# Attention bias of a fused three-stage kernel: two small loads issued ahead of a table, two scalings moved into the first block, 44 instead of 26 warm-up transposes

## The chip, the cores and the metric

The kernel runs on one core of a Trainium2 chip. A core has a matrix engine (TensorE; PE in the profile, with its weight loads as PEld), three elementwise engines (VectorE or DVE, ScalarE or ACT, GpSimd or POOL) and SyncE (SP), which here issues every transfer of the 16 DMA engines. Each engine works through its own instructions in order and waits at semaphores for the others. Matmul operands come from the on-chip memory (SBUF), results go to eight PSUM banks. The metric is the device time of one execution in microseconds (us).

## The reference, cut to what matters

The change lies in the bias of the attention, the first of three stages. Two feed-forward networks follow and are not touched.

```python
B, H, S, D = 2, 8, 576, 64                       # batch, heads, positions, head size; hidden = 32
scores = scale * np.matmul(q, k.transpose(0, 1, 3, 2))
rel = (pos[:, None] - pos[None, :]).astype(np.float32)
psi_rel = np.log1p(np.abs(rel))
psi_i = np.log1p(np.maximum(pos[:, None].astype(np.float32), 1.0))
x = (psi_rel / psi_i)[..., None]
h = np.maximum(x @ w1 + b1, 0.0)
bias = h @ w2                                    # (S, S, H)
scores = scores + bias.transpose(2, 0, 1)[None]
attn = softmax(scores)                           # over the last axis
x = attn @ v, then _moe_ref(x), then _moe2_ref   # the two feed-forward stages
```

## The kernel before

**The bias.** A hidden unit of the bias network is on where `w1*psi_rel > -b1*psi_i`. The kernel therefore keeps a table `lw` with the logarithms of all 1151 distances, one copy per partition shifted for four groups of 32 partitions (4 row offsets times 32 hidden units), and multiplies it once by `w1` (`w1c`, one number per partition). The thresholds `thr` hold `psi_i`, multiplied once by `-b1` (`b1c`). For a group of rows, DVE compares a 576-wide window of `lw` with a column of `thr` and writes a 0/1 mask (L254); every fifth group instead has ACT write the sign (L264, four pieces issued during the four groups before it). PE multiplies the mask with a small matrix `wb` made from `w2`, `w1` and `b1` (eight 128x288 matmuls for a group of two masks, into a PSUM tile `bps` of which there are two), and ACT copies the result to the SBUF tile `ev` (L281, or L279 after a sign group).

**Blocks.** Five blocks of rows run one after another (`bias_rows(t)`, 16 groups each in the first four, 8 in the last). In block 0 the window never reaches below column 496 of `lw`, so only the part from `NEAR = 448` on is needed there. Blocks 1 to 3 need the part below `NEAR` as well, block 4 has a table of its own, `lw8`.

**After a block.** When its last `ev` is written, SP issues 16 transfers (L298) that rearrange `ev` into tiles `ba` and `bc`; DVE multiplies and adds these (L313, L317) between the masks of the next block, at fixed groups (the first one at group 5). The moves of a block wait for its last copy into `ev`.

**The start.** SP issues, in order, the loads of `w1c`, `w2c`, the upper part of `lw` (L119), `b1c`, `thr`, the lower part of `lw` (L122), `lw8` (L123), then the first row scales `xt`, q, k and v. ACT scales the upper part (L135), then the lower part (L141) and `lw8` (L142), before its first copy into `ev`. PE runs 26 transposes of the identity (L94) as soon as the identity exists; their result is not used. DVE and POOL make `wb` from `w1c`, `w2c` and `b1c` (L130 to L140), with DVE scaling `thr` (L136) in between.

**Order.** The schedule is written by hand: the instructions of an engine stand in the order of the code, and a wait of the first holds up all behind it.

Of the kernel before, what the change touches and what calls it, by code (L numbers as in the profile page):

```python
# [14 lines left out]
AF = mybir.ActivationFunctionType  # L15
# [42 lines left out]
def attention_then_two_ffn(ctx: ExitStack, tc: tile.TileContext, q, k, v, w1, b1, w2, w_in, w_out, ca, cb, probs, e_w1, e_w2, c_l, c_l8, c_p, c_x, out):  # L58
    nc = tc.nc
    act, dve, pool, pe, sp = nc.scalar, nc.vector, nc.gpsimd, nc.tensor, nc.sync  # L60

    def f32(ap):
        return ap.bitcast(F32)

    def mm(o, l, r, start, stop):
        pe.matmul(o, lhsT=l, rhs=r, start=start, stop=stop)  # L66
# [21 lines left out]

    ps = ctx.enter_context(tc.tile_pool(name="ps", bufs=2, space=PSUM))

    WARM = 26
    warm = ps.tile([P, 512], F32, tag="o", name="warm")
    for _ in range(WARM):
        pe.transpose(warm[:, :P], ident, ident)  # L94
# [11 lines left out]
    lw = bp.tile([P, LW_W], F32, name="lw")  # L106
    lw8 = bp.tile([P, LW8_W], F32, name="lw8")
# [3 lines left out]
    w1c = bp.tile([P, 1], F32, name="w1c")  # L111
# [3 lines left out]
    NEAR = S - P  # L115
    c_lb = c_l.unsqueeze(1).to_broadcast([4, 32, LW_W])
    sp.dma_start(w1c, w1.unsqueeze(2).to_broadcast([4, HID, 1]))
    sp.dma_start(w2c, w2.unsqueeze(0).to_broadcast([4, HID, H]))
    sp.dma_start(lw[:, NEAR:], c_lb[:, :, NEAR:])  # L119
    sp.dma_start(b1c, b1.unsqueeze(0).unsqueeze(2).to_broadcast([4, HID, 1]))  # L120
    sp.dma_start(thr, c_p.unsqueeze(1).to_broadcast([4, 32, NROWG]))
    sp.dma_start(lw[:, :NEAR], c_lb[:, :, :NEAR])  # L122
    sp.dma_start(lw8, c_l8.unsqueeze(1).to_broadcast([4, 32, LW8_W]))  # L123

# [12 lines left out]
    for par in range(2):  # L137
        for r in range(4):
            rows = slice(32 * r, 32 * r + 32)
            (dve if par == 0 else pool).tensor_copy(wb[rows, par, :, :, :, 4 * par + r], f32(wacr[rows]).rearrange("p a c (q h) -> p a c q h", q=2))  # L140
    act.activation(lw[:, :NEAR], lw[:, :NEAR], AF.Copy, scale=w1c)  # L141
    act.activation(lw8, lw8, AF.Copy, scale=w1c)  # L142

    half = bp.tile([P, 1], F32, name="half")
    ones = bp.tile([P, 1], F32, name="ones")
# [86 lines left out]
    def halves():  # L232
        pool.memset(ones, 1.0)
        for i in range(1, 4):
            pool.tensor_tensor(wsum, f32(wb[:, 0, 0]) if i == 1 else wsum, f32(wb[:, i // 2, i % 2]), ALU.add)
        hs = ps.tile([P, 512], F32, tag="t", name="hs")
        mm(hs[:, :1], wsum.rearrange("p a q r h -> p (a q r h)"), ones, True, True)
        act.activation(half, hs[:, :1], AF.Copy, scale=0.5)

    def bias_rows(t):  # L240

        ng = 16 if t < 4 else 8
        l = lw if t < 4 else lw8
        ev = (ev_odd if t % 2 else ev_even).tile([P, ng, S], F32, tag="ev", name="ev")
        sm = {}

        def window(g, par):
            i0, m = t * P + 4 * ng * par + g, 32 * t + ng * par + g
            return l[:, S - 1 - i0:2 * S - 1 - i0], thr[:, m:m + 1]

        def mask(g, par):
            mk = bp.tile([P, S], F32R, tag="mask", name="mask", bufs=4)
            win, at = window(g, par)
            dve.tensor_scalar(mk, win, at, None, ALU.is_gt)  # L254
            return mk

        def sign(g, i):

            par, hf = divmod(i, 2)
            if hf == 0:  # L260
                sm.setdefault(g, []).append(bp.tile([P, S], F32R, tag="sign", name="sign", bufs=2))
            win, at = window(g, par)
            j = slice(288 * hf, 288 * hf + 288)
            act.activation(sm[g][par][:, j], win[:, j], AF.Sign, scale=-1.0, bias=at)  # L264

        for g in range(ng):

            sc = ps.tile([P, 2, 512], F32, tag="s", name="bps")
            sgn = g in SGN[t]
            ms = sm.pop(g) if sgn else [mask(g, par) for par in range(2)]  # L270
            if t == 0 and g == 3:
                halves()
            for hf in range(2):
                for par in range(2):
                    for part in range(2):
                        mm(sc[:, hf, :288], wb[:, par, part].rearrange("p a q r h -> p (a q r h)"), ms[par][:, 288 * hf:288 * hf + 288], par + part == 0, par + part == 2)
            e_out = ev[:, g].rearrange("p (a j) -> p a j", a=2)
            if sgn:
                act.activation(e_out, sc[:, :, :288], AF.Identity, scale=-0.5, bias=half)  # L279
            else:  # L280
                act.activation(e_out, sc[:, :, :288], AF.Copy)  # L281
            for i in range(4):
                if g + 5 - i in SGN[t]:
                    sign(g + 5 - i, i)

            for f, rows, quad, h, n in WITH.get((t, g), ()):
                f(rows, quad, dve, slice(h, h + n))
        return ev
# [41 lines left out]
    for t in range(5):  # L330
        if t == 4:

            xts[4] = xp.tile([P, S], F32, tag="xt", name="xt")
            ev_ph.close()
            ev_even = ev_ph.enter_context(tc.tile_pool(name="ev_last", bufs=1))
        ev = bias_rows(t)
        if t == 0:
            for e in range(2):
                split_k(e, pool)
        if t < 4:  # L340
            for quad in range(2):
                for ac in range(2):
                    bias_move(t, ev, quad, ac)
        if 0 < t < 3:
            bias_x(t + 1)
# [668 lines left out]
```

## Time and profile before

| what | us |
|---|---|
| median of 3 timed runs (lowest, highest) | 966.3 (966.03, 969.66) |
| the profiled execution, its own time | 963.71 |
| its span, first to last instruction | 961.8 |
| block 0 of the bias: first mask to last copy into `ev` | 11.83 to 37.06 |
| PE busy | 878.7 (91% of the span) |
| DVE / ACT / POOL busy | 550.1 / 463.6 / 202.4 |

The bias takes about the first 145 us, the attention runs to about 345, the feed-forward stages fill the rest with PE nearly always busy. The page's share of busy time is a mean over these stages; the change lies in the first 40 us, where the engines wait for transfers and for each other.

### The profile page before, as it was taken

How to read it: one execution, taken by the hardware profiler on the slowest of the kernel's cores; microseconds unless marked ns; L12 is line 12 of the kernel's file. 1: busy time of each engine (PE TensorE's matmuls, PEld its weight loads, DVE VectorE, ACT ScalarE, POOL GpSimd, SP SyncE). 2: the span in 40 equal slices, each digit the busy share in tenths (PEclk: the TensorE clock that was granted, in tenths of full speed). 3: DMA queues.
4: the chain of work that ended last, by engine and by line, in shares of the span. 5: the costliest groups of instructions: out<-in, count | busy, mean ns of one | idle time of the engine just before them, and what ended most of it. 6: DMA issues, size and time to landing. Idle time of an engine off the chain costs nothing.

```text
span 961.8 us, 13043 instructions
## 1 busy us (share of the span) xinstructions
PE 878.7 (91%) x5012; PEld 821.6 (85%) x5012; DVE 550.1 (57%) x853; ACT 463.6 (48%) x772; POOL 202.4 (21%) x223
## 2 busy tenths in 40 slices
PE   6866876899999979998989989999999999999998
PEld 5865875799888979988989988998899899989987
DVE  3666776688989878888889971222223231331111
ACT  3735554589888767877867742232112111111100
POOL 3000003575554433454733200000000000000000
PEclk7978887799999989999999999999999999999999
DMA  4255556422241312222221122021101210110000
GB/s 103 68 141 145 174 199 195 118 64 65 58 97 29 111 44 88 88 88 88 89 88 44 48 62 68 1 70 62 44 1 64 68 44 1 45 44 12 22 33 33
DMA packets 72552, 69.90 MB, mean 73 GB/s; under 512 B 42412, under 2 KB 51116, under 8 KB 72492
## 3 DMA queue, kind: packets, MB, share of 16 engines
q1 hardware_dynamic: 72492, 69.09, 24.0%
q8 instruction: 39, 0.64, 0.3%
q14 instruction: 21, 0.17, 0.1%
HBM read 45.48 MB, written 2.36 MB: 50 GB/s over the span
## 4 chain that ended last, share of the span: by engine, by line
PE 53%; DVE 18%; DMA 11%; ACT 10%; issue 4%; SPq 3%; POOL 0%; DVEq 0%; ACTq 0%; POOLq 0%
PE hp L66 22%; PE op L66 20%; DMA ba<-ev 8%; PE bps L66 3%; DVE qd L903 2%; DVE narrow L426 2%; PE sc L66 2%; DVE u L904 2%; DVE narrow L424 2%; SPq L298 2%; DVE pq L521 2%; PE o L66 2%; ACT u L899 2%; DVE pt L562 2%; ACT narrow L420 2%
## 5 line engine op out<-in xcount | busy, mean ns | idle before, releaser
L66 PE MATMUL hp<-x,wi 128*128 128x384 f32 x1656 | 294.3, 335 | 13.8 <-DVE u L921 13.7
L66 PEld LDWEIGHTS hp<-x,wi 128*128 128x128 f32 x1656 | 287.3, 188 | 18.5 <-issue 16.7
L66 PE MATMUL op<-w,h_hi 128*128 128x512 f32 (+1 forms) x592 | 178.4, 384 | 0.0
L884 ACT ACTIVATE h_hi<-hp 128x768 fp32r<-128x768 f32 x48 | 39.1, 814 | 245.1 <-PE hp L66 245.1
L885 DVE SCALAR_TENSOR_TENSOR h_lo<-hp,h_hi 128x768 fp32r<-128x768 f32 x48 | 45.9, 957 | 154.9 <-ACT h_hi L884 154.9
L66 PEld LDWEIGHTS op<-w,h_hi 128*128 128x128 f32 x592 | 110.0, 188 | 21.4
L66 PE MATMUL bps<-mask,wb 128*128 128x288 f32 x472 | 84.1, 342 | 38.1 <-DVE mask L254 25.0
L66 PEld LDWEIGHTS bps<-mask,wb 128*128 128x128 f32 x472 | 78.2, 227 | 42.3 <-ACT ev L281 15.4
L66 PE MATMUL op<-w,h_lo 128*128 128x512 f32 (+1 forms) x296 | 113.7, 384 | 0.0
L66 PE MATMUL yp<-g_hi,w 128*128 128x384 f32 x384 | 101.7, 335 | 2.0 <-ACT y L868 1.6
L956 DVE SCALAR_TENSOR_TENSOR acc<-op,pr_sb,acc 128x512 f32<-128x512 f32 (+1 forms) x28 | 20.5, 732 | 112.8 <-PE op L66 112.8
L66 PEld LDWEIGHTS yp<-g_hi,w 128*128 128x128 f32 x384 | 69.7, 188 | 3.1 <-ACT y L868 2.2
L66 PE MATMUL sc<-ks,qs 128*128 128x288 f32 x320 | 64.8, 332 | 7.7 <-DVE nm L521 4.5
L66 PEld LDWEIGHTS op<-w,h_lo 128*128 128x128 f32 x296 | 55.6, 188 | 11.0
L66 PE MATMUL yp<-g_lo,w 128*128 128x384 f32 x192 | 64.2, 334 | 0.0
L254 DVE TENSOR_SCALAR mask<-lw,thr 128x576 fp32r<-128x576 f32 x118 | 56.7, 531 | 13.1 <-PE bps L66 12.3
L281 ACT ACTIVATE ev<-bps 128x576 f32<-128x576 f32 x59 | 38.3, 650 | 49.2 <-PE bps L66 36.4
L66 PEld LDWEIGHTS sc<-ks,qs 128*128 128x128 f32 x320 | 48.7, 203 | 14.2 <-DVE nm L521 8.0
L838 POOL TENSOR_TENSOR g_lo<-u,g_hi 128x768 fp32r<-128x768 f32 x24 | 45.4, 1890 | 70.3 <-ACT g_hi L837 59.3
L521 DVE CUSTOM_DVE_ANT_0 pq<-sc,ba 128x576 f32<-128x576 f32 x72 | 53.8, 749 | 8.2 <-PE sc L66 8.1
L531 ACT ACTIVATE pq<-pq,nm 128x576 f32<-128x576 f32 x72 | 55.4, 769 | 3.4 <-DVE nm L521 3.1
L562 DVE TENSOR_TENSOR pt<-tp,pt 128x512 fp32r<-128x512 f32 x72 | 49.3, 684 | 11.7 <-ACT pt L561 11.1
(130 smaller groups left out, 1276.6 us busy)
## 6 DMA issues: line engine op xcount, KB each, us to landing
stage<-in_moe_w_dram SPq DMA_DIRECT2D x32, 512.0 KB
ba<-ev SPq DMA_DIRECT2D x32, 288.0 KB
bc<-ev SPq DMA_DIRECT2D x32, 288.0 KB
words<-in_moe_w_in_dram SPq DMA_DIRECT2D x7, 1024.0 KB
words<-in_moe_w_out_dram SPq DMA_DIRECT2D x7, 1024.0 KB
raw_q<-in_q_dram SPq DMA_DIRECT2D x32, 128.0 KB
raw_k<-in_k_dram SPq DMA_DIRECT2D x16, 128.0 KB
raw_v<-in_v_dram SPq DMA_DIRECT2D x16, 128.0 KB
```

The costliest lines, as they stand in the source:

```text
L66: pe.matmul(o, lhsT=l, rhs=r, start=start, stop=stop)
L254: dve.tensor_scalar(mk, win, at, None, ALU.is_gt)
L281: act.activation(e_out, sc[:, :, :288], AF.Copy)
L298: sp.dma_start(dst[:, h], ev[r:r + 29:4])
L420: act.activation(st, hi.bitcast(F32), AF.Abs, scale=SHIFT)
L521: dve.tensor_tensor_reduce(out=self.row(u).rearrange("p (a j) -> p a j", a=2), in0=sc[:, :, :288], in1=bs.rearrange("p (a j) -> p a j", a= ...
L531: act.activation(self.row(u), self.row(u), AF.Exp, bias=least.pop((self.n, u)), scale=-1.0, accum_out=self.sm[b][:, u - 4 * b:u - 4 * b + 1])
L562: dve.tensor_tensor(lo, tp, f32(hi), ALU.subtract)
L838: pool.tensor_tensor(lo, u, f32(hi), ALU.subtract)
L884: act.activation(hi, h, AF.Relu)
L885: dve.scalar_tensor_tensor(out=lo, in0=h, scalar=0.0, in1=f32(hi), op0=ALU.max, op1=ALU.subtract)
L956: dve.scalar_tensor_tensor(out=acc[:, j, cols], in0=op, scalar=pr_sb[:, j, e:e + 1], in1=acc[:, j, cols], op0=ALU.mult, op1=ALU.add)
```

## The change

Three edits. The loads of `b1c` and `thr` are issued before the upper part of `lw` instead of after it. The scalings of the lower part of `lw` and of `lw8` leave the start and stand in block 0 behind the copies of groups 9 and 12. The number of warm-up transposes goes from 26 to 44.

```diff
-    WARM = 26
+    WARM = 44
...
     sp.dma_start(w2c, w2.unsqueeze(0).to_broadcast([4, HID, H]))
-    sp.dma_start(lw[:, NEAR:], c_lb[:, :, NEAR:])
     sp.dma_start(b1c, b1.unsqueeze(0).unsqueeze(2).to_broadcast([4, HID, 1]))
     sp.dma_start(thr, c_p.unsqueeze(1).to_broadcast([4, 32, NROWG]))
+    sp.dma_start(lw[:, NEAR:], c_lb[:, :, NEAR:])
     sp.dma_start(lw[:, :NEAR], c_lb[:, :, :NEAR])
...
-    act.activation(lw[:, :NEAR], lw[:, :NEAR], AF.Copy, scale=w1c)
-    act.activation(lw8, lw8, AF.Copy, scale=w1c)
...
                 act.activation(e_out, sc[:, :, :288], AF.Copy)
+            if t == 0 and g in (9, 12):
+                x = lw[:, :NEAR] if g == 9 else lw8
+                act.activation(x, x, AF.Copy, scale=w1c)
             for i in range(4):
                 if g + 5 - i in SGN[t]:
                     sign(g + 5 - i, i)
```

The lines of the code move by two, so L281 of before is L279 of after, and so on. SP's first transfers before (`lw_117` is `lw8`; the last number is the elements per partition):

```order
L117 DMA w1c<-in_w_dram 128x1x1
L118 DMA w2c<-in_w_dram 128x1x8
L119 DMA lw<-in_c_l_dram 128x1x703
L120 DMA b1c<-in_b_dram 128x1x1
L121 DMA thr<-in_c_p_dram 128x1x144
L122 DMA lw<-in_c_l_dram 128x1x448
```

And the same place after:

```order
L117 DMA w1c<-in_w_dram 128x1x1
L118 DMA w2c<-in_w_dram 128x1x8
L119 DMA b1c<-in_b_dram 128x1x1
L120 DMA thr<-in_c_p_dram 128x1x144
L121 DMA lw<-in_c_l_dram 128x1x703
L122 DMA lw<-in_c_l_dram 128x1x448
```

The upper part of `lw` has moved two places back; what follows it keeps its place. ScalarE's first instructions before, from the table load on:

```order
L71 ACT_TABLE_LOAD
L135 ACTIVATE lw<-lw,w1c 128x703
L141 ACTIVATE lw<-lw,w1c 128x448
L142 ACTIVATE lw_117<-lw_117,w1c 128x640
L281 ACTIVATE ev<-bps 128x576
L264 ACTIVATE sign<-lw,thr 128x288
```

In the changed kernel L279 follows L135 at once, and the two scalings stand here, in block 0 from the copy of group 9 on (`lw_135` is `lw8`, L277 the copy of a sign group):

```order
L279 ACTIVATE ev<-bps 128x576
L283 ACTIVATE lw<-lw,w1c 128x448
L277 ACTIVATE ev<-bps,half 128x576
L262 ACTIVATE sign<-lw,thr 128x288
L279 ACTIVATE ev<-bps 128x576
L262 ACTIVATE sign<-lw,thr 128x288
L279 ACTIVATE ev<-bps 128x576
L283 ACTIVATE lw_135<-lw_135,w1c 128x640
L262 ACTIVATE sign<-lw,thr 128x288
L279 ACTIVATE ev<-bps 128x576
L262 ACTIVATE sign<-lw,thr 128x288
```

Two pieces of the sign of group 15 and the copies of groups 13 to 15 now stand behind the scaling of `lw8`.

## Rows read from the trace of the kernel before

**Rows 1.** Chain of waits to 65 us: start us, length us, what.
```profile
18.61 0.64 ACT ev L281
19.30 1.38 PE bps L66 x8
...
37.08 0.71 SPq L298
```

**Rows 2.** Timeline after block 0: start us, us, engine line operation [idle before, releaser].
```profile
43.57 1.36 DVE L313 TENSOR_TENSOR ba<-ba,xt 128x1152 f32<-128x1152 f32 x1 [3.36 <-DMA ba<-ev]
...
129.57 3.50 SPq L298 DMA_DIRECT2D ba<-ev  x4
```

**Rows 3.** Windows: PE, PEld, DVE, ACT, POOL busy us, granted clock, DMA share, GB/s.
```profile
4.00:6.00 2.00, 2.00 (x11) 2.00 (x10) 0.23 (x1) 0.00 (x0) 0.00 (x0) 1.00 0.24 84
...
10.00:12.00 2.00, 0.00 (x0) 0.00 (x0) 1.64 (x9) 0.00 (x0) 1.05 (x5) 0.55 0.94 248
...
50.00:55.00 5.00, 4.97 (x25) 4.93 (x26) 3.39 (x6) 1.72 (x3) 0.00 (x0) 0.66 0.54 142
...
70.00:75.00 5.00, 1.50 (x12) 1.27 (x11) 3.90 (x6) 1.27 (x3) 0.00 (x0) 1.00 0.53 143
...
85.00:90.00 5.00, 3.82 (x27) 3.31 (x25) 2.26 (x4) 3.35 (x6) 0.00 (x0) 1.00 0.53 141
...
150.00:155.00 5.00, 4.24 (x18) 4.21 (x19) 3.51 (x10) 3.19 (x8) 0.75 (x1) 0.51 0.58 200
```

**Rows 4.** Timeline of the start.
```profile
2.14 0.53 SPq L119 DMA_DIRECT2D lw<-in_c_l_dram  x1
...
3.29 0.53 SPq L121 DMA_DIRECT2D thr<-in_c_p_dram  x1
...
8.95 0.88 ACT L135 ACTIVATE lw<-lw,w1c 128x703 f32<-128x703 f32 x1 [6.93 <-DMA lw<-in_c_l_dram]
...
9.97 0.23 DVE L131 TENSOR_SCALAR wac<-w2c,b1c 128x8 f32<-128x8 f32 x1 [5.71 <-DMA b1c<-in_b_dram]
...
10.84 0.29 DVE L136 TENSOR_SCALAR thr<-thr,b1c 128x144 f32<-128x144 f32 x1 [0.22 <-DMA thr<-in_c_p_dram]
...
11.83 1.83 DVE L254 TENSOR_SCALAR mask<-lw,thr 128x576 fp32r<-128x576 f32 x4
...
12.50 4.18 PE L66 MATMUL bps<-mask,wb 128*128 128x288 f32 x16 [5.46 <-DVE mask L254]
...
14.07 0.67 ACT L141 ACTIVATE lw<-lw,w1c 128x448 f32<-128x448 f32 x1 [4.24 <-DMA lw<-in_c_l_dram]
...
17.88 0.83 ACT L142 ACTIVATE lw<-lw,w1c 128x640 f32<-128x640 f32 x1 [3.14 <-DMA lw<-in_c_l_dram]
```

**Rows 5.** Transposes: warm-up (ns min/median/max, first and last start), at 150-160, at 196-200 us.
```profile
L94 PE MATMUL warm<-ident x26: 293/421/475, 1.4 to 6.7; 128*128 128x128 f32 x26
...
L549 PE MATMUL tp<-ident,pq 128*128 128x128 f32 x12 | 3.2, 420 | 0.0
...
L549 PE MATMUL tp<-ident,pq 128*128 128x128 f32 x8 | 1.2, 272 | 0.0
```

**Rows 6.** Timeline of block 0's second part and of PE's waits in block 1.
```profile
20.40 1.80 DVE L254 TENSOR_SCALAR mask<-lw,thr 128x576 fp32r<-128x576 f32 x2 [3.17 <-PE bps L66]
...
25.40 4.50 PE L66 MATMUL bps<-mask,wb 128*128 128x288 f32 x32
...
35.06 1.22 PE L66 MATMUL bps<-sign,wb 128*128 128x288 f32 x8
...
36.31 0.74 ACT L279 ACTIVATE ev<-bps,half 128x576 f32<-128x576 f32 x1 [0.40 <-PE bps L66]
...
45.51 2.46 PE L66 MATMUL bps<-mask,wb 128*128 128x288 f32 x16 [2.85 <-DVE mask L254]
...
50.03 3.45 PE L66 MATMUL bps<-mask,wb 128*128 128x288 f32 x16 [2.06 <-DVE mask L254]
...
83.90 2.46 PE L66 MATMUL bps<-mask,wb 128*128 128x288 f32 x16 [1.27 <-DVE mask L254]
```

## The prediction

> **What bounds the kernel now.** I read the chain of waits first. It runs from the loads of the table through ScalarE's first copy at 18.61 and TensorE's restart at 19.30 to the end of block 0, and from there to the first move at 37.08 [rows 1]. The reader is to see that nothing before 37.08 matters by itself: what counts is when the last copy of block 0 ends, since the moves wait for it.
>
> Then the timeline and the windows after block 0: DVE stands 3.36 us before its first bias product, waiting for a move [rows 2], and the DMA share is 0.53 at 70 to 75 us and at 85 to 90, with TensorE idle most of the first of these [rows 3]. The moves come one behind the other, until those of block 3, issued from 129.57 on [rows 2]. So the bias is paced by its transfers from 37.08 on. If the first move is issued x us earlier, I take the whole of x as gained; the attention and the feed-forward stages then start earlier and are otherwise the same.
>
> Then the timeline of the start. The first mask begins at 11.83: the upper table is there at 8.95 and scaled 0.88 later, but `b1c` comes at 9.97 and `thr` at 10.84 [rows 4], and DVE works on these until the mask. TensorE starts at 12.50. ScalarE waits for the lower table until 14.07 and for `lw8` until 17.88 [rows 4], and only then copies the first group out of PSUM. With two PSUM tiles TensorE stands after two groups (16 matmuls in 4.18 us, to 16.68) until 19.30.
>
> **The first edit: loads.** `b1c` and `thr` now go ahead of the upper table. Both DVE's and POOL's work on `wb` and `thr` then lies under the table's transfer, and the first mask waits for the table alone. Two bounds for its landing. Issued two places later (2.14 to 3.29), it lands 1.15 later, at 10.10. If the three loads pass one behind the other, the three end together when they did before, at 10.84. I take the middle, 10.5: the DMA share of 0.24 at 4 to 6 us [rows 3] says that the table uses a quarter of the 16 DMA engines, which leaves open how much of the two small loads it has to wait for.
>
> The Trainium skill (DMA: Bandwidth & Descriptors, "Why a DMA increments its semaphore by 16 and not by 1") says that a transfer is spread over the largest number of engines up to 16 that divides its slowest dimension; for these loads, with 4 there, that is 4 engines. The trace's 0.24 agrees. By that rule the three share the same queues and the landing is the later bound, which would take 0.35 us off the gain.
>
> From 10.5: 0.88 for the scaling, 0.03 to the mask, and 0.67 from mask to matmul as before (11.83 to 12.50) give 12.08. The gain here is 0.4 us (0 to 0.8). SP's queue behind (the lower table, `lw8`, `xt`, q, k, v) keeps its place.
>
> **The second edit: scalings.** ScalarE copies group 0 as soon as it is done, so TensorE's stand from 16.68 to 19.30 goes. What is late next is TensorE itself. At full clock it went from 25.40 to 35.06 through nine groups [rows 6], 1.073 each, and the last group ended its copy 2.0 after its start (35.06 to 36.31 plus 0.74). 16 groups from 12.08 at that pace: 12.08 + 15 x 1.073 + 2.0 = 30.2.
>
> The scalings are not gone: 0.67 and 0.83 [rows 4] now stand between copies. Their cover is the 0.40 that ScalarE idles before a sign group's copy [rows 6]; two sign groups, 10 and 15, follow, so 0.7 to 1.5 stays. I take 1.3, since two pieces of group 15's sign queue behind the second scaling and TensorE waits for them. The loads of both parts are long there by then. DVE: two masks took 1.80 while POOL split k at the same time [rows 6], against 1.83 for four at the start [rows 4]; that split now falls into a stretch where TensorE is not waiting anyway. 0.3 (0 to 0.7). Sum at full clock: 31.8.
>
> **The third edit: warming.** 18 more transposes cost nothing by themselves, since TensorE has nothing else until 12.08. The question is the clock. The granted clock reads 1.00 at 4 to 6 us [rows 3], yet the transposes there took 421 ns, as those of the attention did at 150 to 160 (420), where the clock was low (0.51 at 150 to 155), and only the last ones came down to 293, near the 272 of the faster ones at 196 to 200 [rows 3, 5]. So I read the start as low clock (1.2 GHz) until about 6.7. The pace was (6.7 - 1.4) / 25 = 0.212 us; the 18 additional ones at half of that end at about 8.7. Then TensorE idles 3.4 us until 12.08.
>
> What the clock did after idle times: it fell at about 10.2 after the idle from 7 (0.55 at 10 to 12); it was low for 0.34 x 2 x 5 = 3.4 us of 50 to 55 after idles of 2.85 and 2.06; it stayed at 1.00 at 85 to 90 after 1.27 [rows 3, 6]. An idle of 3.4 belongs to those that cost a stretch. I take one such stretch of 3.4 us, when the first groups run, and it costs half of it, 1.7 (0 to 3.4).
>
> The Trainium skill (TensorE: Matmul & The Clock Gate, "Part 1: The HAM clock gate (the "warmup" mystery)") says that the throttled clock is the default and that activity lifts it. It contradicts the clock column of the first 6 us, and the durations agree with the skill. By the column alone the 44 transposes would last to 10.7, the idle would be 1.3, and the gain 5.3.
>
> **The sum.** Block 0 ends at 31.8 + 1.7 = 33.5 instead of 37.05: 3.6 us. The profiled execution took 963.71 (its span and 1.9 around it), so 960.1 for it; it was 2.6 faster than the median of the runs, 966.3, and against that the forecast is 962.7.
>
> **Rivals.** *The clock stays up* (the 44 transposes reach far enough). For it: the idle of 1.27 cost nothing [rows 3, 6], and the transposes may last longer than by my pace. Against: 3.4 is longer than any idle of [rows 6]. Gain 3.6 + 1.7 = 5.3: 961.0.
>
> *The earlier end is not passed on*: the moves are limited by DMA from 37 to beyond 130, and some later transfer or wait could decide instead. For it: 92 us lie between the first move and the last block's moves, with many waits. Against: DVE's waits for moves and the steady share of 0.53. Nothing gained: 966.3.
>
> *Slower: the clock in the attention.* TensorE's idle times there end at transfers; the windows at 50 to 55 show what two idles cost. With all starts shifted, low stretches can fall differently between 145 and 190, where TensorE is often on the chain. Four more stretches on the path, priced like the one of 50 to 55 at 1.7 each, cost 6.8; less 3.6, that is 969.5. It makes the kernel slower from three on (5.1 against 3.6); fewer stretches than now are as likely.
>
> **How the numbers follow.** Chances: forecast 0.50 (own range 960.5 to 965, from the bounds above), clock stays up 0.25, not passed on 0.17, slower 0.08. The low end: best bounds (landing 10.1, scalings 0.7, masks and clock 0) give 6.5, 959.8, and a run may lie 2.6 under the median as the profiled one did: 957.5. The high end takes in the case of no gain and a part of the slower one: 967.5. A measurement of this kernel tells about 0.5% (4.8 us) from no change. Beyond 961.5 lie a quarter of the first case and somewhat over half of the second: faster 0.28; slower by that much 0.06; within, 0.66.
>
> **What would show it.** In the profile of the changed kernel: the upper table's scaling at 10.1 to 10.9 and the first mask right behind; no wait of ScalarE for tables after that; TensorE without a stop after the second group; the last warm-up transposes at 272 to 293 ns and ending near 8.7; low clock for one stretch between 11 and 18; the first move at 32 to 35; the later stages shifted by the same amount. It is wrong if the first move comes after 36, or comes at 33 and block 1's first product is not earlier by as much.

## The result and the profile after

| | before | after |
|---|---|---|
| median of the 20 runs (lowest, highest), us | 966.25 (958.9, 971.59) | 962.47 (946.04, 970.61) |
| ratio after to before, 95% interval | | 0.9871 [0.9833, 0.9908] |
| profiled execution: its own time, its span | 963.71, 961.8 | 959.28, 957.4 |
| first mask of block 0 | 11.83 | 12.87 |
| last copy of block 0 ends | 37.05 | 34.33 |
| last matmul of the bias ends | 143.2 | 137.0 |
| first feed-forward matmul | 333.8 | 327.8 |

The median came out 0.2 us from the forecast of 962.7. The ratio shows a larger gain than the medians do (962.47 / 966.25 = 0.9961), because it compares only the runs within 1.5% of each kernel's fastest, 6 of 20 of the changed kernel, three of them at 946 to 949, and all 20 of the kernel before: it tells of those few more than of most executions. These three are what the forecast did not hold, and most of the experiments are about them. With the two repeats below the changed kernel has 7 of 38 runs at 945 to 951, while none of 130 runs of the kernel before, taken beside all experiments, is below 958.8.

First the steps of the prediction, in the timeline of the start after the change (start us, us, engine, line and operation, in brackets the idle time before and what ended it):

```profile
2.14 0.53 SPq L119 DMA_DIRECT2D b1c<-in_b_dram  x1
...
3.28 0.53 SPq L121 DMA_DIRECT2D lw<-in_c_l_dram  x1
...
6.24 0.23 DVE L131 TENSOR_SCALAR wac<-w2c,b1c 128x8 f32<-128x8 f32 x1 [1.98 <-DMA b1c<-in_b_dram]
...
7.10 0.30 DVE L136 TENSOR_SCALAR thr<-thr,b1c 128x144 f32<-128x144 f32 x1 [0.21 <-DMA thr<-in_c_p_dram]
...
11.96 0.88 ACT L135 ACTIVATE lw<-lw,w1c 128x703 f32<-128x703 f32 x1 [9.94 <-DMA raw_q<-in_q_dram]
12.87 1.81 DVE L252 TENSOR_SCALAR mask<-lw,thr 128x576 fp32r<-128x576 f32 x4 [4.80 <-ACT lw L135]
13.54 5.11 PE L66 MATMUL bps<-mask,wb 128*128 128x288 f32 x24 [4.32 <-DVE mask L252]
...
15.71 0.65 ACT L279 ACTIVATE ev<-bps 128x576 f32<-128x576 f32 x1 [2.88 <-PE bps L66]
```

The first edit did what it says: `b1c` is there at 6.24 instead of 9.97 and `thr` at 7.10 instead of 10.84 [rows 4], and the first mask now waits for the table alone. But the table is scaled at 11.96 instead of 8.95, which is 3.0 later, and the first mask starts 1.04 later instead of 0.4 earlier. The releaser that the row names, `raw_q`, is not what the scaling needs; it needs the table and `w1c`.

The second edit did what it says too: ScalarE's first copy is at 15.71 instead of 18.61 [rows 1], and TensorE runs 24 matmuls without a stop. In the second part of block 0 and behind it:

```profile
27.12 0.66 ACT L283 ACTIVATE lw<-lw,w1c 128x448 f32<-128x448 f32 x1
...
30.38 0.82 ACT L283 ACTIVATE lw<-lw,w1c 128x640 f32<-128x640 f32 x1
...
32.22 1.33 PE L66 MATMUL bps<-sign,wb 128*128 128x288 f32 x8 [0.31 <-ACT ev L279]
...
33.59 0.74 ACT L277 ACTIVATE ev<-bps,half 128x576 f32<-128x576 f32 x1 [0.46 <-PE bps L66]
34.35 3.57 SPq L300 DMA_DIRECT2D ba<-ev  x4
...
40.84 1.36 DVE L315 TENSOR_TENSOR ba<-ba,xt 128x1152 f32<-128x1152 f32 x1 [3.35 <-DMA ba<-ev]
```

TensorE waits once, 0.31, for a copy that stands behind the second scaling. The first move is at 34.35 instead of 37.08 [rows 1], the first product at 40.84 instead of 43.57, with the same wait in front of it [rows 2]: the 2.7 us are passed on to block 1.

The transposes and the clock (the group of the warm-up; then windows with the columns of [rows 3]):

```profile
L94 PE MATMUL warm<-ident x44: 272/421/477, 1.4 to 8.9; 128*128 128x128 f32 x44
```

```profile
4.00:6.00 2.00, 2.00 (x11) 2.00 (x10) 0.23 (x1) 0.00 (x0) 0.00 (x0) 1.00 0.10 25
6.00:8.00 2.00, 2.00 (x15) 2.00 (x14) 1.44 (x8) 0.00 (x0) 0.84 (x4) 1.00 0.57 110
8.00:10.00 2.00, 1.22 (x12) 0.98 (x9) 0.07 (x1) 0.00 (x0) 1.57 (x9) 1.00 0.78 195
...
14.00:17.45 3.45, 3.45 (x16) 3.45 (x16) 1.98 (x5) 1.07 (x2) 0.00 (x0) 0.51 0.42 128
```

The median transpose took 421 ns while the column reads 1.00, and 15 transposes in 6 to 8 us against 11 in 4 to 6 tell where the clock came up. They end at 9.2 (forecast 8.7), TensorE stands for 4.32, and the low clock, 0.51, is one stretch of 3.4 at 14.0. The first two windows also show the price of the loads: at 4 to 6 us the DMA engines move 25 GB/s instead of 84 [rows 3], since the table has not begun; and at 8 to 10, `xt` moves beside it.

The chain of waits now begins with the upper table, as forecast, and then goes the old way:

```profile
3.28 8.58 DMA lw<-in_c_l_dram
13.54 5.11 PE bps L66 x24
18.77 11.04 PE bps L66 x80
32.22 1.34 PE bps L66 x8
...
42.57 15.40 DMA ba<-ev
```

The bias ends 6.2 earlier, not 2.7. The other 3.5 lie in blocks 1 to 4, where nothing of the kernel was changed. That is the place to look.

### The profile page after: what moved, and what is told of

It is laid out like the page before. It is cut to its first block, busy times and chain, and to the rows that moved or that the text cites. A ratio compares the mean times of both kernels' runs of the same rounds, so it can differ in the third digit from the quotient of the medians.

```text
span 957.4 us, 13079 instructions
## 1 busy us (share of the span) xinstructions
PE 879.1 (92%) x5030; PEld 822.5 (86%) x5030; DVE 549.6 (57%) x853; ACT 463.3 (48%) x772; POOL 201.5 (21%) x223
## 4 chain that ended last, share of the span: by engine, by line
PE 55%; DVE 19%; ACT 10%; DMA 8%; issue 4%; SPq 3%; POOL 0%; DVEq 0%; ACTq 0%; POOLq 0%
PE hp L66 22%; PE op L66 21%; PE bps L66 4%; DMA ba<-ev 3%; SPq L300 2%; PE sc L66 2%; DVE qd L905 2%; DVE narrow L428 2%; DVE u L906 2%; DVE narrow L426 2%; PE o L66 2%; DVE pq L523 2%; ACT u L901 2%; ACT narrow L422 2%; DMA xt<-in_c_x_dram 2%
## 5 line engine op out<-in xcount | busy, mean ns | idle before, releaser
L66 PEld LDWEIGHTS hp<-x,wi 128*128 128x128 f32 x1656 | 288.9, 189 | 17.6 <-issue 16.2
L66 PE MATMUL bps<-mask,wb 128*128 128x288 f32 x472 | 81.7, 335 | 32.5 <-DVE mask L252 21.2
L66 PEld LDWEIGHTS bps<-mask,wb 128*128 128x128 f32 x472 | 75.8, 220 | 36.5 <-issue 19.2
L66 PEld LDWEIGHTS sc<-ks,qs 128*128 128x128 f32 x320 | 47.9, 200 | 16.8 <-DVE nm L523 10.8
L279 ACT ACTIVATE ev<-bps 128x576 f32<-128x576 f32 x59 | 38.4, 650 | 48.9 <-PE bps L66 36.1
```

## The experiments

Each was timed in five rounds beside the kernel before on the same chip.

**One edit at a time.** The first kernel has the first edit alone, the second the second, the third the third (each by its lines of the diff above).

```diff
-    sp.dma_start(lw[:, NEAR:], c_lb[:, :, NEAR:])
     sp.dma_start(b1c, b1.unsqueeze(0).unsqueeze(2).to_broadcast([4, HID, 1]))
     sp.dma_start(thr, c_p.unsqueeze(1).to_broadcast([4, 32, NROWG]))
+    sp.dma_start(lw[:, NEAR:], c_lb[:, :, NEAR:])
```

> The kernel before with the first edit alone (b1c and thr ahead of the upper table). Theory A (the three loads share their queues, so the table comes later by what stands ahead of it): first mask at 12.5 to 13.0 instead of 11.83, first move 0.5 to 1.5 us later than 37.1, time of the kernel before or up to 1.5 us more. Rival B (the table comes only two issue slots later and DVE's work is hidden): first mask at 11.0 to 11.8, first move 0 to 1 us earlier.

```diff
-    act.activation(lw[:, :NEAR], lw[:, :NEAR], AF.Copy, scale=w1c)
-    act.activation(lw8, lw8, AF.Copy, scale=w1c)
...
+            if t == 0 and g in (9, 12):
+                x = lw[:, :NEAR] if g == 9 else lw8
+                act.activation(x, x, AF.Copy, scale=w1c)
```

> The kernel before with the second edit alone (the two scalings behind the copies of groups 9 and 12). Theory A (TensorE's stand for ScalarE was the cost): TensorE goes on after the second group, first move at 33 to 35 instead of 37.1, so 2 to 4 us less time. Rival B (the warming gives the gain): TensorE starts at 12.5 at low clock, stays there for 4 to 7 us, first move at 35.5 to 37, less than 1.5 us gained.

```diff
-    WARM = 26
+    WARM = 44
```

> The kernel before with the third edit alone (44 transposes). Theory A (the stand for ScalarE until 18.6 stays): first move at 35.5 to 37.1, 0 to 1.5 us gained at most. Rival B (clock is what counts): the first groups run at full clock and the first move comes before 35, 2 us or more gained.

The changed kernel ran again beside them, and once more with the next set:

> The changed kernel once more. Theory A (block 0 ends 2 to 4 us earlier, the rest is the same): median 2 to 5 us under the kernel before, first move at 33 to 35. Rival C (something behind block 0 also differs between executions, by up to 15 us, as the lowest of 20 runs were 946 to 949 and none of the kernel before under 958): one or more of these runs lies at 946 to 951; where the profiled one does, the moves of the bias or the attention take 8 us or more less, at the same first move.

> The changed kernel a third time, for its spread and one more profile. Theory D: 1 to 3 of about 12 runs lie at 945 to 951; where the profiled one does, its attention starts with fewer low stretches and is 8 us or more shorter, while block 0 ends as before at 34. Rival C: the bias is shorter in it, by faster moves.

| kernel | median of the runs, us | ratio [95%] | first mask | block 0 ends |
|---|---|---|---|---|
| loads alone | 964.76 of 12 | 1.0012 [0.9989, 1.0035] | 12.81 | 36.92 |
| scalings alone | 963.86 of 12 | 0.9968 [0.9947, 0.9989] | 11.95 | 33.31 |
| warming alone | 966.63 of 12 | 0.9995 [0.9968, 1.0022] | 11.93 | 37.59 |
| all three again | 961.49 of 12 | 0.9874 [0.9828, 0.9919] | 12.83 | 34.04 |
| all three, second time | 962.07 of 6 | 0.9864 [0.9809, 0.9919] | 13.34 | 35.12 |

The first edit alone shows the same late table, in its timeline:

```profile
11.89 0.88 ACT L135 ACTIVATE lw<-lw,w1c 128x703 f32<-128x703 f32 x1 [9.88 <-DMA lw<-in_c_l_dram]
12.81 1.81 DVE L254 TENSOR_SCALAR mask<-lw,thr 128x576 fp32r<-128x576 f32 x4 [4.71 <-ACT lw L135]
...
19.16 1.53 PE L66 MATMUL bps<-mask,wb 128*128 128x288 f32 x8 [1.88 <-ACT ev L281]
```

TensorE starts later, stands 1.88 for ScalarE's first copy instead of 2.6 (16.68 to 19.30), and goes on at 19.16, as before at 19.30 [rows 1]: alone, the edit is hidden behind the scalings and neither gains nor loses. The table came as late as theory A said, but the first move, at 36.95, is not later than before. With the scalings gone the edit loses: block 0 ends at 34.33, 34.04 and 35.12 with it and at 33.83 without it (next run). The second edit carries the whole gain of block 0, 3.74. Its profile is of the slowest of its twelve runs, 975.53, but what made that one slow lies in the attention (below). The third edit does nothing in block 0: alone its first move is at 37.62, and with the scalings block 0 ends at 33.31 after 26 transposes and at 33.83 after 44. And none of the 36 runs with one edit was below 957.9.

**Old order of the loads with the other two edits, then 80 transposes.**

```diff
+    sp.dma_start(lw[:, NEAR:], c_lb[:, :, NEAR:])
     sp.dma_start(b1c, b1.unsqueeze(0).unsqueeze(2).to_broadcast([4, HID, 1]))
     sp.dma_start(thr, c_p.unsqueeze(1).to_broadcast([4, 32, NROWG]))
-    sp.dma_start(lw[:, NEAR:], c_lb[:, :, NEAR:])
```

> The changed kernel with the loads in the old order: second and third edit. Theory A (the first edit costs a microsecond, the second gives the gain, the third a part of a low stretch): first mask at 11.8 to 12.0, first move at 32 to 34, median 1 us under the changed kernel, 960 to 962. Theory D (runs of 945 to 950 come where the bias or the attention meets the clock differently, and any earlier start can do it): some of the runs lie at 945 to 951 here too. Rival E (they need the first edit): none does.

```diff
-    WARM = 44
+    WARM = 80
```

> As the kernel before it, with 80 transposes, which reach to the first matmul: no idle of TensorE between them. Theory A (the idle after the 44 costs a stretch of low clock, 1.7 us): no low clock in block 0 after the transposes, first move at 31.5 to 32.5, 1 to 2 us less time than with 44. Rival B (the clock of the first groups is not what sets block 0's end): first move as with 44, within 0.5 us.

With 44: median 961.09 of 12, ratio 0.9848 [0.98, 0.9897], first mask 11.92, block 0 ends at 33.83, two runs at 945.9 and 949.6. With 80: median 960.14 of 9, lowest 952.1, ratio 0.9933 [0.9901, 0.9965], block 0 ends at 32.67. The windows of the latter show no low clock from the last transposes to the end of block 0; the first two of them:

```profile
10.00:14.00 4.00, 3.61 (x30) 3.25 (x29) 3.45 (x13) 0.61 (x1) 2.78 (x9) 1.00 0.76 194
14.00:18.00 4.00, 3.75 (x29) 3.52 (x28) 3.25 (x7) 3.25 (x7) 2.12 (x5) 1.00 0.45 129
```

The transposes end at 12.23, TensorE goes on at 12.62, and the granted clock stays at 1.00, the level of 2.4 GHz. In each of the profiles with 44 transposes, where TensorE idles for 3.5 to 5.8 before the first matmul, a low stretch follows. So the idle time decides, as far as these runs tell and as forecast, and 44 is too few.

At full clock block 0 takes 20.05 from the first matmul, 1.95 over 15 x 1.073 + 2.0. Two later profiles with 80 transposes (both staggered versions below), also without a low stretch there, take 20.59 and 20.57. The scalings and masks thus come to 1.95 to 2.5; the forecast was 1.6. With the scalings, 44 transposes and a low stretch of 3.4 block 0 takes 20.54 to 21.24 in three profiles, with one of 6.8 it takes 21.02 to 21.72 in six (in the staggered ones and their controls the small loads come only after block 0). By the means the low clock costs 0.5 or 0.9, against a forecast of 1.7, and profiles of one kind differ by as much as that. TensorE makes good a part of it within the block: 8 us after its first matmul it has done 46 in the changed kernel and 53 in each of the three profiles with 80 transposes, after 12 us 74 against 76 to 80.

**Is it the attention?** Transposes without use, put between the first six attention units, keep TensorE busy there.

```diff
+            if n == 0 and u < 6:
+                for _ in range((6, 6, 26, 6, 12, 6)[u]):
+                    pe.transpose(warm[:, :P], ident, ident)
```

> The changed kernel with 62 more unused transposes of the identity in the first six units of the attention, where TensorE idles at transfers (26 of them ahead of the longest idle). Theory D (what differs between executions is the clock at the attention's start): the low stretches between 140 and 180 go, the time from the first score matmul to the first feed-forward matmul falls from 186 to 178 or less, and most runs lie at 945 to 953. Rival F (transfers pace that part, not the clock): the low stretches go, the attention takes 184 to 188 as before, median 960 to 964.

Median 961.02 of 12, ratio 0.9797 [0.9747, 0.9846]: as the changed kernel. But its profile caught one of its two short runs, 950.0. From its first attention transpose to the first feed-forward matmul it took 197.0 us, not less than the changed kernel's 191.0, although the low clock between 137 and 182 us fell from 24 to 17 us. Its bias ended at 121.6 instead of 137.0. So this short run is short in the bias. There the products of DVE, which wait for the moves, stand closer. The changed kernel's timeline, every product of one stretch:

```profile
62.04 1.36 DVE L315 TENSOR_TENSOR ba<-ba,xt 128x1152 f32<-128x1152 f32 x1 [0.98 <-DMA ba<-ev]
...
66.01 1.36 DVE L319 TENSOR_TENSOR ba<-ba,bc 128x1152 f32<-128x1152 f32 x1 [0.89 <-DMA bc<-ev]
...
69.97 1.36 DVE L319 TENSOR_TENSOR ba<-ba,bc 128x1152 f32<-128x1152 f32 x1 [0.88 <-DMA bc<-ev]
```

The same in the run of 950.0:

```profile
52.41 1.36 DVE L319 TENSOR_TENSOR ba<-ba,bc 128x1152 f32<-128x1152 f32 x1 [0.66 <-DMA bc<-ev]
...
55.30 1.36 DVE L315 TENSOR_TENSOR ba<-ba,xt 128x1152 f32<-128x1152 f32 x1 [0.66 <-DMA ba<-ev]
...
58.30 1.36 DVE L315 TENSOR_TENSOR ba<-ba,xt 128x1152 f32<-128x1152 f32 x1
```

4.0 us apart in the one, 3.0 in the other. The windows tell it without a search: the moves go at 141 to 151 GB/s or at about 200, with the DMA share at 0.53 either way. The changed kernel (both), and behind it the run of 950.0:

```profile
50.00:55.00 5.00, 3.40 (x20) 3.17 (x19) 3.11 (x4) 2.90 (x6) 0.00 (x0) 0.84 0.53 143
...
110.00:115.00 5.00, 5.00 (x40) 4.99 (x39) 4.79 (x8) 4.56 (x9) 0.00 (x0) 1.00 0.53 201
```

```profile
55.00:65.00 10.00, 6.46 (x47) 5.94 (x45) 9.70 (x16) 4.95 (x10) 0.00 (x0) 1.00 0.52 197
```

The kernel before has both paces as well, 142 at 50 to 55 [rows 3] and this, which the prediction did not look at:

```profile
110.00:115.00 5.00, 5.00 (x31) 5.00 (x30) 4.48 (x8) 3.04 (x7) 0.00 (x0) 0.74 0.54 204
```

In the records of single packets (2304 bytes each) the median, taken over 6 us at a time, is 122 to 152 ns in the slow pace of these two kernels and 95 in the fast one. The share of 0.53 means that about half of the 16 engines are at work, in both; most of the time eight such packets are under way at once, in both.

An execution can change its pace more than once, and it does so without the change too. The profiles of the loads alone and of the warming alone end block 0 no earlier than the kernel before (36.92 and 37.59), yet the bias at 137.8 and 138.2 instead of 143.2. The warming alone has the fast pace early and then the slow one again:

```profile
55.00:60.00 5.00, 3.07 (x21) 2.51 (x19) 3.60 (x7) 2.24 (x4) 0.00 (x0) 1.00 0.52 195
...
75.00:80.00 5.00, 2.46 (x16) 2.19 (x16) 3.57 (x7) 2.20 (x5) 0.00 (x0) 1.00 0.53 132
```

So the 3.5 us that the changed kernel's profile gained in blocks 1 to 4 are no more than the pace alone can give.

**Out of step.** Theory: the engines that share a move run in step and get into each other's way, until something puts them out of step. Two small loads, of no use, after the second move of blocks 0 to 3, should do that if they load the engines unevenly (meant: 32 rows over two engines, 96 over six), and not if they are spread evenly over eight (the control, with `(64, 8, 8), (0, 8, 8)`). The packet records do not name the engine. That the two kinds fall differently on the engines shows in their time: the 128 packets of the first pair start over 0.87 us, those of the control over 0.49 (in the second version of both, below).

```diff
+    jam = xp.tile([P, 112], F32, tag="jam", name="jam", bufs=1)
...
             sp.dma_start(dst[:, h], ev[r:r + 29:4])
+            if (quad, ac, h) == (0, 0, 1):
+                for p0, m, k in ((96, 2, 16), (0, 6, 16)):
+                    sp.dma_start(jam[p0:p0 + m * k], c_x[0:m, 0:112].unsqueeze(1).to_broadcast([m, k, 112]))
```

> The changed kernel with two small loads more (32 rows over two DMA engines, 96 rows over six, 448 bytes each, into an unused tile), issued after the second move of each of blocks 0 to 3, so that the engines that share the moves no longer run in step. Theory G (the moves run slowly, at 135 ns for a packet, because the engines stay in step and collide; once out of step they stay at 95 ns): bias products of DVE 3.0 us apart from block 0 or 1 on, the bias ends 10 to 15 us earlier than at 136.96, median 945 to 953, most runs under 952. Rival H (the pace is drawn anew by something else in each execution, and these loads don't reach it): as the changed kernel, median 960 to 963, 0 to 3 runs of 12 at 945 to 951, first products 4.1 us apart.

> Control of the run before: the same two small loads at the same places, the same bytes, but each spread evenly over eight engines (64 and 64 rows), so that no engine is put ahead of another. Theory G: nothing is put out of step, so as the changed kernel, median 960 to 963 with 0 to 3 runs of 12 at 945 to 951. Rival J (any extra load among the moves is enough to change the pace): like the staggered kernel, median under 953. Rival H: as the changed kernel, and the staggered one too.

> The old order of the loads, the two scalings in block 0, 80 transposes, and the staggering loads of the first of these runs. Theory G: block 0 ends at 32.7 (no low clock in it), the moves are fast from there, bias ends at about 120, median 941 to 950, under both kernels by 10 us or more. Rival H: as without the staggering loads, 957 to 962.

> The kernel before the change with the staggering loads alone. Theory G: the pace of the moves has nothing to do with the change, so the bias ends 10 to 15 us earlier than at 143.2 and the median is 949 to 957 (966 less 10 to 15). Rival K (the change, by its earlier end of block 0, is what makes the fast pace possible): 965 to 967 as without the loads, no run under 955.

| kernel | median, us | ratio [95%] | bias ends | attention, to the first feed-forward matmul |
|---|---|---|---|---|
| changed, staggered | 959.55 of 12 | 0.9936 [0.9909, 0.9963] | 125.9 | 205.4 |
| changed, even (control) | 971.36 of 12 | 1.0045 [1.0006, 1.0083] | 139.8 | 202.3 |
| old loads, 80 transposes, staggered | 957.08 of 9 | 0.9913 [0.9886, 0.9941] | 120.7 | 204.8 |
| before, staggered | 962.87 of 12 | 0.9967 [0.9942, 0.9992] | 127.0 | 203.7 |

As for the totals, both theories missed. The stages part two effects. The bias ended 11.1 earlier than in the changed kernel and 16.2 earlier than in the kernel before with the staggering loads, and not with the even ones; and the attention took 11 to 14 longer in all four than in the changed kernel and the kernel before (191.0 and 190.7). The waits of the attention in the staggered kernel (timeline of ScalarE) name the reason:

```profile
163.25 0.60 ACT L567 ACTIVATE pt<-tp 128x512 fp32r<-128x512 f32 x1 [29.60 <-DMA raw_v<-in_v_dram]
```

It is the first write of `pt` in the attention, and `raw_v` is no input of it. In the program that copy waits for eight DMA queues besides TensorE, in the changed kernel for TensorE alone: the new tile `jam` had moved all later tiles, so that the first `pt` came to lie where earlier transfers had to end first. That was a mistake of the experiment, which hid its own effect.

**The same, with the tile above all others**, where it moves none:

```diff
-    jam = xp.tile([P, 112], F32, tag="jam", name="jam", bufs=1)
...
     ev_even = ev_ph.enter_context(tc.tile_pool(name="ev_even", bufs=1))
+    jam = ev_ph.enter_context(tc.tile_pool(name="jam", bufs=1)).tile([P, 112], F32, name="jam")
```

> The staggered kernel again, with the buffer of the two small loads above all other tiles, so that no later tile changes its place and the first attention unit no longer waits for block 4's last moves (29.6 us in the first version, 205 us from the first transpose of the attention to the first feed-forward matmul instead of 191). Theory G (engines in step make the slow pace): bias ends at about 126, attention 191 to 197, median 945 to 953 and most of the 12 runs in it, the profiled one with products 3.0 us apart. Rival H (the pace was drawn by chance in the three staggered profiles): median 959 to 963, as the changed kernel.

> Its control: the same bytes spread evenly over eight engines, buffer above all other tiles. Theory G: as the changed kernel, median 960 to 964, at most 3 of 12 runs at 945 to 951, products 4.1 us apart in blocks 0 and 1. Rival J (any load among the moves changes the pace): 945 to 953, as the staggered one.

> Old order of the loads, scalings in block 0, 80 transposes and the staggering loads, buffer above all other tiles. Theory G: bias ends at about 121, attention 191 to 197, median 940 to 947, below both kernels in every run. Rival H: 957 to 961.

> The kernel before the change with the staggering loads alone, buffer above all other tiles. Theory G: bias ends at about 127 instead of 143.2, median 948 to 956, and the first two blocks with products 3.0 us apart. Rival K (only an earlier end of block 0 makes the fast pace possible): 965 to 967, no run below 955.

| kernel | median (lowest, highest), us | ratio [95%] | block 0 ends | bias ends | attention |
|---|---|---|---|---|---|
| changed, staggered | 949.52 (946.25, 952.42), 6 | 0.9812 [0.9759, 0.9865] | 35.21 | 126.4 | 193.3 |
| changed, even (control) | 962.24 (949.42, 972.18), 12 | 0.991 [0.9864, 0.9957] | 34.66 | 139.8 | 195.5 |
| old loads, 80 transposes, staggered | 946.01 (943.59, 949.57), 6 | 0.9779 [0.9726, 0.9832] | 33.24 | 124.2 | 192.9 |
| before, staggered | 951.36 (946.24, 953.24), 6 | 0.9821 [0.9767, 0.9875] | 37.01 | 130.1 | 190.1 |

DVE's groups of 40 to 100 us (count, busy, mean ns; then idle time before them) in the changed kernel, staggered:

```profile
L319 DVE TENSOR_TENSOR ba<-ba,xt 128x1152 f32<-128x1152 f32 x10 | 13.6, 1357 | 8.9 <-DMA ba<-ev 8.8
L323 DVE TENSOR_TENSOR ba<-ba,bc 128x1152 f32<-128x1152 f32 x8 | 10.8, 1354 | 1.9 <-DMA bc<-ev 1.9
```

And in the control:

```profile
L319 DVE TENSOR_TENSOR ba<-ba,xt 128x1152 f32<-128x1152 f32 x8 | 10.9, 1358 | 15.0 <-DMA ba<-ev 15.0
L323 DVE TENSOR_TENSOR ba<-ba,bc 128x1152 f32<-128x1152 f32 x6 | 8.1, 1358 | 8.4 <-DMA bc<-ev 8.4
```

The first `pt` waits for nothing but TensorE now (ScalarE's timeline of the staggered one):

```profile
135.89 0.60 ACT L567 ACTIVATE pt<-tp 128x512 fp32r<-128x512 f32 x1
```

Of the groups the reader is to see 18 products against 14 in the same 60 us, and 10.8 us of waiting for moves instead of 23.4. The windows of 45 to 55 us, staggered and then the control, agree:

```profile
45.00:55.00 10.00, 8.44 (x52) 7.67 (x51) 7.73 (x12) 6.00 (x11) 0.00 (x0) 0.90 0.52 201
```

```profile
45.00:55.00 10.00, 8.64 (x42) 8.09 (x40) 5.60 (x9) 5.23 (x10) 0.00 (x0) 0.62 0.53 139
```

This shows three things. First, the same bytes in all make the moves fast when they fall unevenly on the engines and leave them slow when they fall evenly, so it is not the load as such. Only one uneven and one even pattern were tried, and the two loads of a pair differ in size in the one (96 and 32 rows) and not in the other.

Second, every run of the three staggered kernels lies below every run of the kernel before, so the pace alone is enough for the short runs; the control behaves as the changed kernel, with one of its 12 runs at 949.4. Third, the kernel before, staggered, gets the same: the fast pace needs nothing of the change.

That the engines run in step is the theory that led to the test, and it is not shown. In the packet records of 50 to 85 us, 40% of the control's packets took 92 to 110 ns and 44% took 160 to 190; of the staggered kernel's, 90% took 92 to 110. So in the slow pace there are quick packets and packets that take almost twice as long. But packets start within 3 ns of the one before them about as often in both (20% and 18%), which does not speak for a step. What makes the slow packets slow stays open.

At the fast pace the change itself is worth 951.36 - 949.52 = 1.8 us, and block 0 ends 37.01 - 35.21 = 1.8 earlier in the two profiles; with six runs each, spread over 6 to 7 us, the first of these is no more than a hint. The version with the old order of the loads, both scalings in block 0, 80 transposes and the staggering loads is the fastest, 20.4 us below the median of the kernel before beside it (966.37).

## Why the prediction came out as it did

**The step that failed: "So the bias is paced by its transfers from 37.08 on. If the first move is issued x us earlier, I take the whole of x as gained; the attention and the feed-forward stages then start earlier and are otherwise the same."** The first half held: the first product moved with the first move. What failed is that the transfers were taken to have one pace. They have two, 141 to 151 and about 200 GB/s. For each of the 16 bias products of blocks 0 and 1 that is 4.0 or 3.0 us, and the bias ended 15.4 us earlier in the one execution with the fast pace nearly throughout (121.6 against 137.0). Seven of 38 executions of the changed kernel are 11 to 17 us under its median of 962.47; an execution of the filled kernel that short had the fast pace from the second product on. The forecast had no case at 946, and its range ended at 957.5. The page could have told: the share of 0.53 was read as a steady stream, and the GB/s beside it (143 at 70 to 75 [rows 3], 204 at 110 to 115) as nothing.

*Why the change brings an execution into the fast pace more often than before* is not settled. Scalings with 44 transposes did it with either order of the loads (2 of 12 with the old one), while 0 of 36 runs with one edit alone came below 957.9. All of these begin their moves at 33 to 35 or at 37. An early start alone is not enough: the scalings alone begin them at 33.34 and had no short run in 12. That the start of the moves against something else decides is a guess that no run tested.

**The first edit, mis-sized:** 1.04 us lost instead of 0.4 gained, and the landing at 11.96, outside both bounds (10.10, 10.84). The later bound assumed that three loads end together when they did before. In the packet records the table begins at 6.05 instead of 3.46 and ends at 10.97 instead of 8.55, and `thr` began only at 4.87, after an issue at 2.71. I read this as the table waiting for the two small loads and for `thr`'s own start, which lay under the table before; no run parts the two. Then 0.99 pass from its last packet to the scaling, where it was 0.40; `xt` moves at that time, but no run tested that.

The rule of the Trainium skill (DMA: Bandwidth & Descriptors, "Why a DMA increments its semaphore by 16 and not by 1"), by which these loads share the same four engines, had pointed to the later of the two bounds; the trace went further the same way.

**The second edit, right:** block 0 gained 3.74 alone; 1.95 to 2.5 came back for scalings and masks, forecast 1.6.

**The third edit, right on the mechanism, too dear by size:** a low stretch of 3.4 or 6.8 came after the idle time, and by the means it cost 0.5 or 0.9 us in place of 1.7. That 44 instead of 26 saves nothing there was not in the forecast, which priced the clock without asking what 26 would cost beside the scalings (33.31 for block 0).

**The sum:** 2.7 us at the end of block 0 instead of 3.6 (3.0 and 1.9 in the two repeats). That the median came within 0.2 us of the forecast is in part luck: the late table and the cheaper clock were off in opposite directions, and what the rest of the bias gave and the later stages took was not in the sum. The low end of the range, 957.5, is 957.2 by its own terms (959.8 less 2.6), which changes nothing. The profiled execution gained 4.4 in span: 2.7 there, 3.5 in the rest of the bias, 0.2 lost in the attention, and 1.6 lost in the feed-forward stages (957.4 - 327.8 against 961.8 - 333.8), for which no run shows a cause.

**The rivals:** the clock did not stay up. "Not passed on" is refuted by the first product. The slower one, by four more low stretches in the attention, was not seen. Something near it was: the profile of the scalings alone (975.53) has one wait of 20 us in the attention, for a load,

```profile
167.06 1.30 PE L191 MATMUL tp_q<-ident,raw_q 128*128 128x128 f32 x5 [20.00 <-DMA raw_q<-in_q_dram]
```

with the low clock from 149 to 173. There the time goes to the load and the clock falls in its wake, and why that load came late was not tested.

## What to carry to other kernels

Read the GB/s beside the DMA share in every stage: the same share at two rates is a resource with two paces, and its spread between executions can be larger than the change under study. Loads that are moved ahead of a large one can push it back by more than the issue time that they take: here its last packet came 2.4 us later, for 1.1 us of issue. And an experiment that adds a tile must show that no other tile has moved: here that cost 9 to 12 us of the median and hid the effect.

## What the runs showed of the hardware that was not expected

- Transfers from one part of SBUF to another on half of the DMA engines run at about 145 or about 200 GB/s with the same busy share of 0.53, and stay in a pace for tens of microseconds; what decides between them without such help is open. Two loads of 56 KB together after a move, unevenly spread, bring the fast one (201 GB/s at 45 to 55 us), evenly spread they don't (139).
- A transposition at low clock took about 420 ns (0.51 granted at 150 to 155 us) and at full clock 272, while the granted clock of the first microseconds reads 1.00 throughout, with the median of 44 warm-up transposes at 421 and that of 80 at 273.
